# One strided DMA for four in collecting the FFN rows, and the one-hot pieces two and three steps sooner

## The chip, the cores and the metric

The kernel runs on one core of a Trainium2 chip. The metric is the device time of one execution in microseconds, as the median of several runs; the kernel before was run five times. The profile is of one further execution of the same program. Its span runs from the first to the last instruction and is a little shorter than the time of that execution.

The core has five engines with a queue of instructions each, which they work off in order: TensorE (PE in the profile, with its weight loads as PEld), VectorE (DVE), ScalarE (ACT), GpSimd (POOL) and SyncE (SP), which here only issues DMAs. An instruction that needs the result of another engine waits at the head of its queue, and everything behind it on that engine waits too.

## The reference, cut to what matters

`x` is 2048 x 1024 in bfloat16. The output mixes two branches with a gate per row: a linear attention with softmax features over 32 heads of 32 (`a`), and `x` itself with one row changed (`b`). That one row is the row of `x` with the largest routing score `x @ w_r`; a gated feed-forward network (FFN) of width 3584 is applied to it alone.

```python
# attention branch
pq, pk = q @ w_phi, k @ w_phi                                 # per head
phi_q = concat([softmax(pq), softmax(-pq)]); phi_k = concat([softmax(pk), softmax(-pk)])
kv = einsum("bhsf,bhsd->bhfd", phi_k, v); z = phi_k.sum over s
o = einsum("bhqf,bhfd->bhqd", phi_q, kv) / (phi_q . z + 1e-6)
a = o @ wo
# routed branch
r = x @ w_r;  idx = argmax(r)
y = (silu(x[idx] @ w_gate) * (x[idx] @ w_up)) @ w_down * sigmoid(r[idx])
b = x;  b[idx] += y
# mix
g = sigmoid((x * gate_w).sum(-1));  out = g * a + (1 - g) * b
```

## The kernel before, in words

The work goes in three stages.

In the first (to about 70 us) `x` is transposed, `v` is computed (`k_v`, L540), and the per-head matrix `w_phi` is folded into the weights of `q` and `k` (`fold`, L310). `route` finds the row for the FFN.

The second, the k stage (about 70 to 153 us), is a loop written out over `i`, here called steps. Steps 0 to 31 each take one unit `u = i` (128 rows, half of the heads). `k_s0(u)` does eight matmuls `pk` (L582) on PE, two exponentials into a tile `e` on ACT (L585, L586), a sum `ssum` (L590) and reciprocals `rs` (L592) on DVE, a running sum `ksum` on POOL (L594), and the product `phi` (L597), which is on DVE where `u % 4 == 3` and on POOL otherwise. `k_kv(u)` follows five steps later (`LAG`): eight short matmuls `kvps` on PE (L606) that need `phi(u)`. There are four buffers of `e` and six of `phi`. After step 31 the first tiles `pq` of the third stage (L631) take the place of `pk`; they share two PSUM buffers with it. ACT must have read a `pk` or `pq` tile before PE can use its buffer again.

Between these units lie the pieces of the FFN, each at a step given by a number:

- Rounds 0 to 3 of `ffn_gu` (steps 8, 14 and 21, with rounds 2 and 3 both at 21) load gate and up weights through SP (L454) and multiply them with the chosen row: `facc`, L478, leaves four rows of 512 at partitions 0, 32, 64 and 96. ACT copies them to `gs` (L483), and SP sends them to the tile `gT` (L486), in which every row of 512 becomes four rows of 128.
- `ffn_turn(0)` to `(3)` (steps 13, 18, 26 and 27; L439, L442) transpose `gT` by small f32 matmuls into a corner of the PSUM tile `small_ps`. `ffn_mid` (step 27) makes the hidden vector `hh` from it: an exponential on ACT (L446), then L447 to L450 on DVE. `hh32` is its spread copy on ACT (L767, emitted at step 31), which stands on ACT before the exponentials of unit 31.
- `ffn_down` (step 35, L494) multiplies `hh32` with the seven chunks of `w_down`, whose loads (L434) go through SP as soon as buffers are free.
- `one_hot` (step 16: L360 to L367), `one_hot_cols` (step 21: one matmul L372 on PE, then L374 to L385 on DVE) and `one_hot_sums` (step 26: one matmul L390 on PE, then L391 to L397 on DVE) turn the index of the chosen row into a column mask `oh`, the sums `c8` and a clipped index `ixu`, which POOL reads into a register (L831). L372 reads `hlb`, written by L364. L390 reads `csb`, written by L385. L372, L390, L439 and L442 all write parts of the one PSUM tile `small_ps`, and L374 and L391 read it on DVE. The scheduler puts a wait between such an access and the next write of the tile.

The third stage (153 us to the end) computes `pq`, the numerators (`num`, L652), their division on DVE and POOL, the transposes by DMA and the output matmuls (`po`, L709).

The order of the instructions on each engine comes from the Tile scheduler, which interleaves the pieces of neighbouring steps on DVE; the semaphores are set by it too. SP's DMAs take eight completion semaphores in turn, and a DMA whose semaphore is still in use by the DMA eight places before waits for that one to land.

Of the kernel before, what the change touches and what calls it, by code (L numbers as in the profile page):

```python
# [167 lines left out]
def kernel(  # L168
# [4 lines left out]
    nc = tc.nc  # L173
# [54 lines left out]
    gT = const.tile([P, P], F32, name="gT")  # L228
# [85 lines left out]
    def gates():  # L314
        eg = const.tile([P, NT], F32, name="eg")
        nc.scalar.activation(out=eg[:], in_=rg[:, 1, :], func=ACTF.Exp, scale=-1.0)
        nc.vector.tensor_scalar_add(out=eg[:], in0=eg[:], scalar1=1.0)
        nc.vector.reciprocal(out=gate[:], in_=eg[:])
        nc.vector.tensor_scalar(out=omg[:], in0=gate[:], scalar1=-1.0, scalar2=1.0, op0=ALU.mult, op1=ALU.add)
# [117 lines left out]
    def ffn_turn(r):  # L437
        if r < 3:
            nc.tensor.matmul(ffn_ps[:, 16 * r:16 * r + 16], lhsT=gT[:], rhs=identf[:, 0:16], start=True, stop=True)  # L439
        else:  # L440
            for h in range(2):
                nc.tensor.matmul(ffn_ps[:, 48:56], lhsT=gT[:], rhs=identf[:, 16 + 8 * h:24 + 8 * h], start=(h == 0), stop=(h == 1))  # L442
# [9 lines left out]
    def gu_load(r, kp, where):  # L452
        def part(w, a0, src, k0, nk, col, n):
            nc.sync.dma_start(out=w[:, a0:a0 + nk * n * 512].rearrange("p (k f) -> p k f", k=nk) if n == 4 or nk == 4 else  # L454
                              w.rearrange("p (k f) -> p k f", k=2)[:, :, a0:a0 + n * 512],
                              in_=src[:, k0:k0 + nk, col * 512:(col + n) * 512])
        w = wbuf(where)
        gate_load(w[0:1, 0:1])
        k0 = 2 * kp
        if r == 0:  # L460
            part(w, 0, wg_v, k0, 2, 0, 4)
        elif r == 1:
            part(w, 0, wg_v, k0, 2, 4, 3)
            part(w, 1536, wu_v, k0, 2, 0, 1)
        elif r == 2:
            part(w, 0, wu_v, k0, 2, 1, 4)
        else:
            part(w, 0, wu_v, 4 * kp, 4, 5, 2)
        return w

    def ffn_gu(r, bufs):
        ws = [gu_load(r, k, b) for k, b in enumerate(bufs)]
        acc = psB.tile([P, 512], F32, name="facc", tag="pB")
        for k, w in enumerate(ws):
            for q in range(2):
                for g in range(4):
                    kb = 4 * k + 2 * q + g // 2 if r == 3 else 2 * k + q
                    nc.tensor.matmul(acc[32 * g:32 * g + 32, :], lhsT=xs32[:, kb, :],  # L478
                                     rhs=w[:, (q * 4 + g) * 512:(q * 4 + g + 1) * 512], start=(k == 0 and q == 0),
                                     stop=(k == len(ws) - 1 and q == 1),  # L480
                                     tile_position=(0, 32 * g), skip_group_check=True)
        gs = wk.tile([P, 512], F32, name="gs", tag="junk", bufs=2)
        nc.scalar.copy(out=gs[:], in_=acc[:])  # L483
        g0 = 16 if r == 3 else 0
        for g in range(4):
            nc.sync.dma_start(out=gT[g0 + 4 * g:g0 + 4 * g + 4, :], in_=gs[32 * g:32 * g + 1, :])  # L486

    def ffn_down(cs_, pools):
        ws = [wd_load(c, p) for c, p in zip(cs_, pools)]
        for bl in range(4 * len(cs_)):  # L490
            blk = cs_[0] * 4 + bl
            for n in range(2):
                g = (bl % 2) * 2 + n
                nc.tensor.matmul(small_ps[32 * g:32 * g + 32, :], lhsT=hh32[:, blk, :],  # L494
                                 rhs=ws[bl // 4][:, bl % 4, n * 512:(n + 1) * 512], start=(blk < 2),
                                 stop=(blk >= NFB - 2), tile_position=(0, 32 * g), skip_group_check=True)

    def moe_cols():
        ym = ring.tile([P, D * 2], F32, name="ym", tag="wch")
        ys = ym[:, 0:512]  # L500
        y4 = ym[0:KB, 512:768].rearrange("p (s c) -> p s c", s=2)
        yrow = ym[0:1, 768:1280].bitcast(BF)
        ybc = ym[:, 1280:1792].bitcast(BF)
        moe["ybc"] = ybc
        nc.scalar.copy(out=ys, in_=small_ps[:])
        for g in range(4):
            nc.sync.dma_start(out=y4[4 * (g % 2):4 * (g % 2) + 4, g // 2, :], in_=ys[32 * g:32 * g + 1, :])
        moe["y4"] = y4
        moe["yrow"] = yrow
# [67 lines left out]
    def k_s0(u):  # L577
        t, hf = divmod(u, 2)
        pk = psA.tile([P, HH, DH], F32, name="pk", tag="pA")
        pkf = pk[:].rearrange("p h f -> p (h f)")  # L580
        for kb in range(KB):
            nc.tensor.matmul(pkf, lhsT=xT[:, kb, t * P:(t + 1) * P], rhs=wkf[:, kb, hf * 512:(hf + 1) * 512],  # L582
                             start=(kb == 0), stop=(kb == KB - 1))
        e = wk.tile([P, HH, 2, DH], BF, name="e", tag="e", bufs=4)
        nc.scalar.activation(out=e[:, :, 0, :], in_=pk[:], func=ACTF.Exp)  # L585
        nc.scalar.activation(out=e[:, :, 1, :], in_=pk[:], func=ACTF.Exp, scale=-1.0)  # L586
        moe["e"] = e
        e2 = e[:].rearrange("p h s f -> p (h s) f")
        ssum = sm.tile([P, HH * 2], F32, name="ssum", tag="ssum")
        nc.vector.tensor_reduce(out=ssum[:], in_=e2, axis=AX.X, op=ALU.add)  # L590
        rs = sm.tile([P, HH * 2], F32, name="rs", tag="rs")
        nc.vector.reciprocal(out=rs[:], in_=ssum[:])  # L592
        moe["rs"] = rs
        nc.gpsimd.tensor_tensor(out=ksum[:], in0=ksum[:], in1=ssum[:], op=ALU.add)  # L594
        phi = wk.tile([P, HH, 2, DH], BF, name="phi", tag="phi", bufs=6)
        eng = nc.vector if u % 4 == 3 else nc.gpsimd
        eng.tensor_tensor(out=phi[:].rearrange("p h s f -> p (h s) f"), in0=e2,  # L597
                                in1=_bc(rs[:], [P, HH * 2, DH]), op=ALU.mult)
        kst[u] = phi

    def k_kv(u):
        t, hf = divmod(u, 2)
        phi = kst.pop(u)
        for pl in range(NPU):
            pr = hf * NPU + pl
            nc.tensor.matmul(kv_slot(pr),  # L606
                             lhsT=phi[:, 2 * pl:2 * pl + 2, :, :].rearrange("p h s f -> p (h s f)"),
                             rhs=v_all[:, t, hf * HH + 2 * pl:hf * HH + 2 * pl + 2, :].rearrange("p h d -> p (h d)"),
                             start=False, stop=(t == NT - 1), skip_group_check=True)
# [14 lines left out]
    def q_front(sb, j):  # L624
        if j == 0:
            ep = w16 if sb % 2 == 0 else qp["eb"]
            est[sb] = ep.tile([P, KB, 2, SB], BF, name="E", tag="w16" if sb % 2 == 0 else "E")
        E = est[sb]
        pq = psA.tile([P, SB], F32, name="pq", tag="pA")
        for kb in range(KB):  # L630
            nc.tensor.matmul(pq[:], lhsT=wqf[:, kb, j * P:(j + 1) * P], rhs=xT[:, kb, sb * SB:(sb + 1) * SB],  # L631
                             start=(kb == 0), stop=(kb == KB - 1))
        nc.scalar.activation(out=E[:, j, 0, :], in_=pq[:], func=ACTF.Exp)  # L633
        nc.scalar.activation(out=E[:, j, 1, :], in_=pq[:], func=ACTF.Exp, scale=-1.0)
# [124 lines left out]
    for i in range(NU + LAG):  # L759
        if i in GU:  # L760
            r = GU.index(i)
            ffn_gu(r, ("AAAD", "DWVA", "AADD")[r])
            if r == 2:
                ffn_gu(3, "WV")
        if i == NU - 1:
            nc.scalar.copy(out=hh32[0:1, 0, 0:1], in_=moe["e"][0:1, 0, 1, 0:1])
            nc.scalar.copy(out=hh32[:], in_=hh[:].unsqueeze(2).to_broadcast([P, NFB, 32]))  # L767
        if i == DN:
            ffn_down(range(7), "AAADDWV")
            moe_cols()  # L770
        if i >= NU and i - NU < NPRE:
            q_front(0, i - NU)
        if i >= LAG:
            k_kv(i - LAG)
        if i < NU:
            k_s0(i)
        if i == 2:
            gates()
        if i in TU:
            ffn_turn(TU.index(i))  # L780
            if i == TU[3]:
                ffn_mid()
        if i == 6:
            xs_turn()
        if i == 16:
            one_hot()
        if i == 21:
            one_hot_cols()
        if i == 26:
            one_hot_sums()  # L790
    qp["eb"] = None
    kv_finish(range(8), nc.vector.tensor_copy)
# [9 lines left out]
    i = 0  # L802
    while i < n_front + NL + 2 or wq_:
# [3 lines left out]
        if 0 <= n < NU:  # L807
            sb, r = divmod(n, 8)
# [63 lines left out]
```

## Time and profile before

| | |
|---|---|
| median of 5 runs | 278.61 us (278.2 to 279.08) |
| profiled execution | 278.27 us, span 276.6 us, granted TensorE clock 1.000 |
| PE busy | 270.6 us (98% of the span) |
| DVE, POOL, ACT busy | 189.5 us (69%), 141.8 us (51%), 119.2 us (43%) |
| DMA, mean over the span | 173 GB/s, 47.97 MB |

In the profile, "busy" is the time in which an engine has an instruction in execution. A line of a timeline gives the start, the duration, the engine, the line of the kernel, the operation, the written and read tiles and their shapes, how many instructions were merged into it, and in brackets how long the engine had been idle and what ended that. SPq lines are DMA issues on SyncE's queue. Records overlap a little where an instruction starts before the last one has drained, so the distance between starts is often the better measure of what one costs.

### The profile page before, as it was taken

What the parts mean: (1) busy time and instruction counts of PE and PEld (TensorE: products, weight loads), DVE (VectorE), ACT (ScalarE), POOL (GpSimd) and SP (SyncE); (2) the same over time, 40 slices, a digit from 0 to 9 for tenths busy, and PEclk for the clock granted to TensorE, in tenths of its full rate; (3) what the DMA queues carried; (4) which work ended last, traced back from release to release, by engine and by line L of the source; (5) the groups of instructions that cost most, each with busy time, mean ns of one, the idle gap of its engine ahead of it and who ended that gap; (6) DMA issues with size and microseconds to landing.
All of it is one profiled execution on the core that took longest, in us unless ns stands there. A gap on an engine that the chain in (4) does not pass through costs nothing.

```text
span 276.6 us, 5433 instructions
## 1 busy us (share of the span) xinstructions
PE 270.6 (98%) x2023; PEld 149.6 (54%) x2023; DVE 189.5 (69%) x392; ACT 119.2 (43%) x227; POOL 141.8 (51%) x152
## 2 busy tenths in 40 slices
PE   8999999999999999999999999999999999999993
PEld 3666667676544555555454555555455545555442
DVE  3020025556899897999992788888776668899862
ACT  3143332323364646546463647844544554232300
POOL 8000000000097978947953079999756655788310
PEclk9999999999999999999999999999999999999999
DMA  7899999977953797649900528743897255426632
GB/s 257 209 171 191 175 193 293 165 148 217 366 220 107 261 347 280 235 153 339 394 24 4 172 62 298 178 93 13 30 169 214 71 116 118 119 89 140 146 99 63
DMA packets 68767, 47.97 MB, mean 173 GB/s; under 512 B 51376, under 2 KB 56576, under 8 KB 68736
## 3 DMA queue, kind: packets, MB, share of 16 engines
q1 hardware_dynamic: 68240, 47.10, 65.8%
q10 hardware_dynamic: 464, 0.48, 0.5%
q8 instruction: 17, 0.28, 0.4%
q14 instruction: 14, 0.11, 0.1%
q0 software_dynamic: 32, 0.00, 0.0%
HBM read 31.00 MB, written 4.20 MB: 127 GB/s over the span
## 4 chain that ended last, share of the span: by engine, by line
PE 92%; DVE 4%; issue 1%; DMA 1%; ACT 0%; DVEq 0%
PE pq L631 20%; PE po L709 20%; PE pv L540 18%; PE pk L582 16%; PE num L652 6%; PE pW L310 3%; PE kvps L606 3%; PE facc L478 2%; DVE ssum L590 2%; PE pv L562 1%; DMA xs_t<-in_A_x_dram 1%; PE kvps L562 1%; PE small_ps L494 1%; DVE hlc L375 1%; PE pT L291 0%
## 5 line engine op out<-in xcount | busy, mean ns | idle before, releaser
L582 PE MATMUL pk<-wkf,xT 128*128 128x512 bf16 x256 | 60.4, 379 | 0.0
L631 PE MATMUL pq<-xT,wqf 128*128 128x512 bf16 x256 | 60.3, 379 | 0.0
L709 PE MATMUL po<-wo_sb,oT 128*128 128x512 bf16 (+2 forms) x264 | 58.8, 373 | 0.0
L681 POOL TENSOR_TENSOR U<-T 128x512 f32<-128x512 f32 x32 | 41.5, 1297 | 32.1 <-DVE T L666 16.9
L540 PE MATMUL pv<-wv_sb,xT 128*128 128x256 bf16 (+2 forms) x336 | 52.9, 307 | 0.0
L597 POOL TENSOR_TENSOR phi<-e,rs 128x1024 bf16<-128x1024 bf16 x24 | 45.8, 1911 | 2.4 <-DVE rs L592 0.9
L709 PEld LDWEIGHTS <-oT 128*128 128x128 bf16 x264 | 25.4, 98 | 27.8
L590 DVE TENSOR_REDUCE ssum<-e 128x32 f32<-128x1024 bf16 x32 | 38.0, 1191 | 2.8 <-ACT e L586 2.6
L540 PEld LDWEIGHTS <-xT 128*128 128x128 bf16 x336 | 31.5, 97 | 14.6
L666 DVE TENSOR_TENSOR T<-num,rq 128x1024 f32<-128x1024 f32 x32 | 38.8, 1213 | 0.0
L547 ACT CAST v_all<-pv 128x384 bf16<-128x384 f32 (+1 forms) x45 | 20.1, 447 | 41.8 <-PE pv L540 36.0
L631 PEld LDWEIGHTS <-wqf 128*128 128x128 bf16 x256 | 23.8, 98 | 24.1 <-issue 0.6
L712 DVE SCALAR_TENSOR_TENSOR o_out<-po,gate,xg 128x512 bf16<-128x512 f32 (+2 forms) x33 | 23.9, 728 | 17.6 <-PE po L709 16.5
L582 PEld LDWEIGHTS <-xT 128*128 128x128 bf16 x256 | 23.0, 97 | 22.8
L682 POOL TENSOR_TENSOR o_sb<-U,rden 128x512 bf16<-128x512 f32 x32 | 33.5, 1048 | 2.5
L585 ACT ACTIVATE e<-pk 128x512 bf16<-128x512 f32 x32 | 19.1, 597 | 31.0 <-PE pk L582 22.7
L633 ACT ACTIVATE E<-pq 128x512 bf16<-128x512 f32 x32 | 19.0, 595 | 29.2 <-PE pq L631 28.8
L420 POOL COPY wch<-wT 1x1 bf16<-1x1 bf16 x3 | 0.4, 176 | 56.8 <-DMA wT<-in_A_wqkv_dram 56.8
L594 POOL TENSOR_TENSOR ksum<-ksum,ssum 128x32 f32<-128x32 f32 x32 | 14.0, 437 | 22.2 <-DVE ssum L590 17.1
L652 PEld LDWEIGHTS <-E 128*128 128x128 bf16 x256 | 16.4, 98 | 9.3 <-DVE T L666 5.4
L652 PE MATMUL num<-KV,E 128*128 128x136 bf16 x256 | 20.5, 223 | 0.0
L586 ACT ACTIVATE e<-pk 128x512 bf16<-128x512 f32 x32 | 18.9, 591 | 0.0
(137 smaller groups left out, 253.6 us busy)
## 6 DMA issues: line engine op xcount, KB each, us to landing
wch<-in_B_w_down_dram SPq DMA_DIRECT2D x7, 1024.0 KB
wch<-in_B_w_up_dram SPq DMA_DIRECT2D x6, 1024.0 KB
wch<-in_B_w_gate_dram SPq DMA_DIRECT2D x4, 1024.0 KB
xin<-in_A_x_dram SPq DMA_DIRECT2D x16, 256.0 KB
out_dram<-o_out SPq DMA_DIRECT2D x30, 128.0 KB
wch<-in_B_w_gate_dram SPq DMA_DIRECT2D x4, 768.0 KB
wv_sb<-in_A_wqkv_dram SPq DMA_DIRECT2D x8, 256.0 KB
wo_sb<-in_A_wo_dram SPq DMA_DIRECT2D x1, 2048.0 KB
```

The costliest lines, as they stand in the source:

```text
L540: nc.tensor.matmul(pv[:, 0:hi - lo], lhsT=xT[:, kb, t * P:(t + 1) * P], rhs=wv_sb[:, kb, lo:hi], start=(kb == 0), stop=(kb == KB - 1))
L547: nc.scalar.copy(out=v_all[:, t, h0:h1, 0:DH], in_=pv[:, 0:(h1 - h0) * DH].rearrange("p (h d) -> p h d", d=DH))
L582: nc.tensor.matmul(pkf, lhsT=xT[:, kb, t * P:(t + 1) * P], rhs=wkf[:, kb, hf * 512:(hf + 1) * 512], start=(kb == 0), stop=(kb == KB - 1))
L590: nc.vector.tensor_reduce(out=ssum[:], in_=e2, axis=AX.X, op=ALU.add)
L597: eng.tensor_tensor(out=phi[:].rearrange("p h s f -> p (h s) f"), in0=e2, in1=_bc(rs[:], [P, HH * 2, DH]), op=ALU.mult)
L631: nc.tensor.matmul(pq[:], lhsT=wqf[:, kb, j * P:(j + 1) * P], rhs=xT[:, kb, sb * SB:(sb + 1) * SB], start=(kb == 0), stop=(kb == KB - 1))
L652: nc.tensor.matmul(num[:, b * NSTR:b * NSTR + KVW], lhsT=E[:, j, sg, tl * P:(tl + 1) * P], rhs=KV[hf][:, sg, jl, :], start=True, stop=True)
L666: nc.vector.tensor_tensor(out=T[:].rearrange("p s (j h) d -> p (s j) h d", h=4), in0=nv[:, :, :, 0:DH], in1=rS.unsqueeze(3).to_broadcast([ ...
L681: nc.gpsimd.tensor_tensor(out=U[:], in0=T[:, 0], in1=T[:, 1], op=ALU.add)
L682: nc.gpsimd.tensor_tensor(out=st["o"][:, hf * HH:(hf + 1) * HH, :], in0=U[:], in1=_bc(rden[:], [P, HH, DH]), op=ALU.mult)
L709: nc.tensor.matmul(po[:, 0:w], lhsT=st["oT"][:, kb, :], rhs=moe["wo"][:, kb, sl], start=(kb == 0), stop=(kb == KB - 1))
L712: nc.vector.scalar_tensor_tensor(out=o_out[:, 0:w], in0=po[:, 0:w], scalar=gate[:, t:t + 1], in1=st["xg"][:, sl], op0=ALU.mult, op1=ALU.add)
```

## The change

Two things are edited. In `ffn_gu`, rounds 1 to 3 send their four rows to `gT` by one DMA whose source steps over partitions 0, 32, 64 and 96; round 0 keeps four DMAs of one row each. `one_hot_cols` moves from step 21 to step 19, and `one_hot_sums` from step 26 to step 23. The number of matmuls and of instructions on DVE, ACT and POOL stays the same; SP issues nine DMAs fewer. From L486 on, every line number in the changed file is one higher.

```diff
@@ -482,8 +482,9 @@
         gs = wk.tile([P, 512], F32, name="gs", tag="junk", bufs=2)
         nc.scalar.copy(out=gs[:], in_=acc[:])
         g0 = 16 if r == 3 else 0
-        for g in range(4):
-            nc.sync.dma_start(out=gT[g0 + 4 * g:g0 + 4 * g + 4, :], in_=gs[32 * g:32 * g + 1, :])
+        step = 4 if r >= 1 else 1
+        for g in range(0, 4, step):
+            nc.sync.dma_start(out=gT[g0 + 4 * g:g0 + 4 * (g + step), :], in_=gs[32 * g:32 * (g + step):32, :])
 
     def ffn_down(cs_, pools):
         ws = [wd_load(c, p) for c, p in zip(cs_, pools)]
@@ -784,9 +785,9 @@
             xs_turn()
         if i == 16:
             one_hot()
-        if i == 21:
+        if i == 19:
             one_hot_cols()
-        if i == 26:
+        if i == 23:
             one_hot_sums()
     qp["eb"] = None
     kv_finish(range(8), nc.vector.tensor_copy)
```

## The prediction

> **What bounds the kernel now.** I read the page's busy row first, then the chain of waits, then the timeline of each engine through the k stage.
>
> ```profile
> PE 270.6 (98%) x2023; PEld 149.6 (54%) x2023; DVE 189.5 (69%) x392; ACT 119.2 (43%) x227; POOL 141.8 (51%) x152
> ```
>
> PE is busy for 98% of the span at full clock. Only a PE idle stretch that goes, or a new one, can move the end. The chain of waits runs along PE everywhere after the start except from 120.5 to 132.9 us, where it follows DVE from L374 to L391 and comes back to PE at L442. PE's timeline shows the one hole there:
>
> ```profile
> 111.37 0.29 PE L439 MATMUL small_ps<-identf,gT 128*128 128x16 f32 x2
> 111.51 0.41 PE L606 MATMUL kvps<-v_all,phi 128*128 128x66 bf16 x8
> ...
> 130.19 0.29 PE L439 MATMUL small_ps<-identf,gT 128*128 128x16 f32 x2
> 130.33 0.16 PE L390 MATMUL small_ps<-csb,const-bfloat16-1.0 128*128 128x2 bf16 x1
> 130.36 0.41 PE L606 MATMUL kvps<-v_all,phi 128*128 128x66 bf16 x8
> 130.61 1.89 PE L582 MATMUL pk<-wkf,xT 128*128 128x512 bf16 x8
> 132.94 0.61 PE L442 MATMUL small_ps<-identf,gT 128*128 128x8 f32 x4 [0.44 <-DVE c L391]
> 133.41 0.41 PE L606 MATMUL kvps<-v_all,phi 128*128 128x66 bf16 x8
> ```
>
> L442 (step 27) writes `small_ps`, which L391 (step 26) has to read first. L391 stands on DVE behind two sums; L390, whose result it copies, starts at 130.33, so DVE is 2.4 us behind PE here. DVE's lines, then POOL's:
>
> ```profile
> 112.97 0.51 DVE L364 CAST hlb<-hl 1x2 bf16<-1x2 uint32 x1
> ...
> 116.95 1.76 DVE L597 TENSOR_TENSOR phi<-e,rs 128x1024 bf16<-128x1024 bf16 x1
> ...
> 120.69 1.71 DVE L375 TENSOR_TENSOR hlc<-hlc,iot 128x1 f32<-128x1 f32 x1
> ...
> 131.68 1.16 DVE L590 TENSOR_REDUCE ssum<-e 128x32 f32<-128x1024 bf16 x1
> 132.75 0.13 DVE L391 COPY c<-small_ps 8x2 f32<-8x2 f32 x1
> 132.94 0.35 DVE L592 RECIPROCAL rs<-ssum 128x32 f32<-128x32 f32 x1
> ```
>
> ```profile
> 111.55 1.91 POOL L597 TENSOR_TENSOR phi<-e,rs 128x1024 bf16<-128x1024 bf16 x1 [0.23 <-PE pk L582]
> ...
> 113.64 1.91 POOL L597 TENSOR_TENSOR phi<-e,rs 128x1024 bf16<-128x1024 bf16 x1
> ...
> 115.72 1.91 POOL L597 TENSOR_TENSOR phi<-e,rs 128x1024 bf16<-128x1024 bf16 x1
> ...
> 120.47 1.91 POOL L597 TENSOR_TENSOR phi<-e,rs 128x1024 bf16<-128x1024 bf16 x1 [0.23 <-PE small_ps L372]
> ```
>
> L375 handles one element per partition and takes 1.71 us: it ends at 122.40, when POOL's `phi` ends (120.47 + 1.91 = 122.38). L364 ends at 113.48, with the `phi` that ends at 113.46. DVE's `phi` at 116.95 ends 1.08 after POOL's (115.72 + 1.91 = 117.63), though the same form needs only 1.15 where POOL is idle (138.40). So some DVE forms wait for the end of a POOL operation, and get in before the next one.
>
> **Part one, the DMAs.**
>
> ```profile
> 102.18 2.48 SPq L486 DMA_DIRECT2D gT<-gs  x4
> ...
> 118.14 5.00 SPq L486 DMA_DIRECT2D gT<-gs  x8
> 123.23 4.80 SPq L434 DMA_DIRECT2D wch<-in_B_w_down_dram  x5
> ```
>
> One issue takes 0.57 to 0.73 us. Round 1 frees SP 2.48 - 0.6 = 1.9 us sooner. For rounds 2 and 3 SP sends one at 118.14, waits for the second `gs` (118.39 + 0.59 = 118.98) and sends the other, so the five `w_down` loads start at about 119.7, 3.5 us sooner. Nobody waits for any of it. `gT` of round 1 is read at 111.37, 7 us after the last issue; rounds 2 and 3 at 130.19, 7 us after. L494 uses `w_down` at 147.36, while DMA is at 0.72 of its time in 134 to 141 us (5 us of it, so loads end near 139) and at 0.01 in 141 to 153: 8 us of cover. A strided DMA of 16 rows isn't in the trace. Between the 0.57 of one row and the 1.24 of a transposing issue I take 0.6; in either case the cover holds, and the price is 0. Nor do its new waits cost: round 1's DMA now waits for round 0's landings, which write the same rows (issued 88.2 to 90.8, over 11 us earlier), round 2's for round 1's (15 us earlier). With nine DMAs fewer, later ones wait for other predecessors on their semaphore (two `w_down` loads for round 3's weights, which `facc` has read by then; the fifth for the load issued at 105.8). Price 0; bounds 0 and, if one load waited for such a neighbour, still 0 by the 8 us.
>
> **Part two, the pieces moved.** The built order of the changed kernel tells where each lands.
>
> *The hole at L442 goes.* L390 and L391 now stand at step 23, and L391 is done near 125, so L442 no longer waits for it. Without a wait L442 starts 1.73 after its `pk` (as 109.64 to 111.37): 130.61 + 1.73 = 132.34. Its four records take 0.28, as two take 111.51 - 111.37 = 0.14, so `kvps` starts at 132.62 in place of 133.41: **-0.79**. The chain's own step (132.94 - 132.34 = 0.60) is the lower bound.
>
> *L372 two steps sooner.* It now follows the `pk` of step 19, so it could start at 113.49, where `kvps` starts now, but needs `hlb`, which L364 ends at 113.48. DVE to PE takes 0.06 (L391 ends 132.88, L442 at 132.94): 113.54. Behind it PE has weight loads of `kvps` that it could not start ahead; eight take 0.32 after the unhindered L372 and 0.50 otherwise. Bounds 0.03 and 0.3; I take **+0.1**, near the first, since the wait itself is 0.05. L390 at step 23 needs `csb` (near 121) at 124.3: 0.
>
> *DVE around step 19.* L374 to L385 came at 120.5 to 125.0, while `facc` of rounds 2 and 3 (2.7 us of PE, no DVE) had let DVE catch up. Now they come at 114.9. L375 waits for POOL's `phi` to end at 115.55, not 1.7 us but 0.2. L376 follows (0.3), then L378, also a product of two SBUF tiles, meets the next `phi` (115.72 to 117.63): 1.7 us lost there. The sum of unit 19 is behind it, at 117.7 in place of 115.30. Then POOL has nothing to do, since its next `phi` needs the sum of unit 20, so L379 goes free and DVE's `phi` takes 1.15, not 1.76. Unit 20's `rs` comes at 122.0 (before 119.94), unit 21's at 123.5 (before 124.58), because the one-hot work is behind DVE by then. POOL's `phi` of unit 20 ends near 124.4, 1.6 before its `kvps` loads (126.0); units 21 and 22 near 126.5 and 128.6, 1.5 before theirs. No wait on PE: 0. If all three products each lost a `phi`, 1.0 to 1.4 us of lag would go on to `kvps` of unit 24 and cost up to 0.5; that is my upper bound.
>
> The Trainium skill (SBUF — State Buffer, section on the two separate sides) calls the port pair of VectorE and GpSimd an exclusive lock, held for a whole instruction, with the loser blocked. It speaks against this move: taken alone, each of L375, L378, L379 put beside a busy POOL costs up to the 1.91 of a `phi`, 5.7 us of DVE, against 1.9 by the rows above, since POOL itself runs dry behind the blocked DVE.
>
> *L395 and POOL's L831* (reads `ixu` from L397). L395 now stands right after unit 24's `rs`, and POOL's `phi` needs 0.17 after that `rs`, so L395 gets in: 0.15. L397 ends near 133, L831 comes after `phi` of unit 25, near 136: 0.
>
> *After the hole.* PE runs 0.7 sooner into POOL's products. `phi` of units 24 to 26 end 1.5 before their `kvps` now; with DVE and POOL 0.4 sooner themselves and PE 0.7, 1.2 is left. What is late next is ACT:
>
> ```profile
> 140.94 0.94 ACT L767 COPY hh<-hh 128x896 bf16<-128x896 bf16 x1
> ...
> 142.28 0.59 ACT L586 ACTIVATE e<-pk 128x512 bf16<-128x512 f32 x1
> ```
>
> `pq` at 143.31 needs the buffer that this L586 frees at 142.87. At 143.31 - 0.7 = 142.61 it would wait 0.3, unless L767, which waits for L447 to L450 on DVE, comes sooner too. DVE is 0.4 ahead, and free of L395's 0.71, so I expect 0, bound 0.3. Then PE sets the pace to the end.
>
> **Sum** against the profiled execution: -0.79 + 0.1 = -0.7, 278.27 to 277.6 (span 275.9). The median of the runs is 0.34 above the profiled one, so the median goes from 278.61 to **277.9**.
>
> **Rivals.**
>
> *Thinner covers take half.* The blocked products hold DVE for longer, or L447 misses its gap between two POOL operations, and PE waits 0.3 at `pq` or up to 0.5 at `kvps` of unit 24 to 26. For it: POOL's cycle of four steps (three `phi` at 2.08, and a fourth turn lost to DVE's) is as long as PE's four steps (4 x 1.98), so lag isn't made up. Against: the margins of 1.2. Time: 278.61 - 0.7 + 0.35 = 278.3.
>
> *Nothing changes.* L442 finds another late predecessor, and the chain goes back to DVE: 278.6. Against: in the built order L442 has no wait on DVE left, and the next matmul's is for `phi` of unit 23, done near 130.
>
> *Slower: L372 waits a whole `phi`.* If POOL's next `phi` (113.64) gets in ahead of L364, `hlb` comes at 113.64 + 1.91 = 115.55, and PE idles 2.1 us at step 19: 278.61 - 0.8 + 2.1 = 279.9. It decides if L364 comes to DVE 0.2 us later. For it: L364 had 6.8 us of cover at step 21 and has none now. Against: nothing in front of L364 is changed, and in this trace it got in. A milder form is L395 losing to the `phi` of unit 24 (2 us of DVE lag, some 1.3 on PE): 279.2.
>
> **How the numbers follow.** About 0.2% (0.56 us) can be told from no change. Full gain 0.55, half 0.22, nothing 0.10, slower 0.13. The full gain of 0.7, within 0.6 to 0.8, passes 0.56 in some three of four runs of the comparison, so faster 0.45; the rest of it, half and nothing make same 0.42; slower 0.13. The range starts at 277.5 (0.79, and the runs' own scatter) and goes to 279.0, over the half and nothing cases and the scatter; 279.2 and beyond is left out. The likeliest case's own range is 277.5 to 278.2.
>
> **What would show it.** Right: L442 starts 1.73 after its `pk` with no idle; L375 short and L378 some 1.9 long near 115.7; three single L486 issues, `w_down` issued from about 119.7, and L494 not moved by it; all of PE after step 27 sooner by 0.7. Wrong: a PE idle before L372 or behind it near 113.5 of over 0.3, before `kvps` of units 20 to 26, or before the second `pq`; or L442 idle again.

## The result and the profile after

The changed kernel takes 277.58 us in the median of 31 runs (276.93 to 278.97), beside 278.57 us for the kernel before in 53 runs (278.04 to 279.56). The ratio is 0.997 with a 95% interval of 0.9962 to 0.9978: 0.84 us faster, between 0.6 and 1.06. The profiled execution took 277.36 us with a span of 275.7 us, against 278.27 and 276.6 before. From L486 on, line numbers are one higher than before wherever the DMA loop has its added line.

The busy row and the chain of waits of the changed kernel, from its page:

```profile
PE 270.6 (98%) x2023; PEld 149.9 (54%) x2023; DVE 189.7 (69%) x392; ACT 119.3 (43%) x227; POOL 140.8 (51%) x152
...
PE 97%; DMA 1%; ACT 0%; DVE 0%; issue 0%
```

PE is busy for the same 270.6 us. In the chain PE had 92% before and DVE 4%; now DVE has 0%. The timeline of PE shows why (start, duration, engine, line):

```profile
111.46 0.29 PE L439 MATMUL small_ps<-identf,gT 128*128 128x16 f32 x2
111.60 0.41 PE L607 MATMUL kvps<-v_all,phi 128*128 128x66 bf16 x8
111.85 1.89 PE L583 MATMUL pk<-wkf,xT 128*128 128x512 bf16 x8
113.63 0.16 PE L372 MATMUL small_ps<-hlb,const-bfloat16-1.0 128*128 128x2 bf16 x1
113.66 0.41 PE L607 MATMUL kvps<-v_all,phi 128*128 128x66 bf16 x8
...
130.75 1.89 PE L583 MATMUL pk<-wkf,xT 128*128 128x512 bf16 x8
132.48 0.51 PE L442 MATMUL small_ps<-identf,gT 128*128 128x8 f32 x4
132.84 0.41 PE L607 MATMUL kvps<-v_all,phi 128*128 128x66 bf16 x8
...
142.75 1.89 PE L632 MATMUL pq<-xT,wqf 128*128 128x512 bf16 x8
```

L442 starts 132.48 - 130.75 = 1.73 after its `pk`, with no idle in front of it; before it was 2.33. From that `pk` to `kvps` PE takes 2.09 in place of 2.80: -0.71. With L372 in front of it `kvps` starts 113.66 - 111.85 = 1.81 after its `pk`; the same pair was 1.73 apart before (111.76 and 113.49): +0.08. From L439 at step 18 to the second `pq` it is 142.75 - 111.46 = 31.29 against 143.31 - 111.37 = 31.94 before: **-0.65**. All of that stands at the end: the last additions into `o_out` start 271.15 - 111.46 = 159.69 after L439, against 160.36 before. This stretch will serve as the measure of PE below, since it is free of what an execution adds at its start and end. With nothing in it edited it came out at 31.95 in the first experiment (31.94 before); but the changed kernel, run again without an edit, gave 31.38, so differences under 0.1 us say little.

What is left of the 0.9 between the two spans lies behind the last additions: from their start to the end of the span it took 276.6 - 271.73 = 4.87 before and takes 275.7 - 271.15 = 4.55 now. The last three experiments ask what that is.

DVE of the changed kernel around step 19, then POOL beside it:

```profile
113.07 0.51 DVE L364 CAST hlb<-hl 1x2 bf16<-1x2 uint32 x1
...
115.39 0.26 DVE L375 TENSOR_TENSOR hlc<-hlc,iot 128x1 f32<-128x1 f32 x1
115.69 2.06 DVE L376 TENSOR_SCALAR oh<-iot,hlc 128x16 f32<-128x16 f32 x1
117.78 0.18 DVE L378 TENSOR_TENSOR oh<-oh,er 128x16 f32<-128x16 f32 x1
...
119.00 0.17 DVE L379 TENSOR_TENSOR oh<-oh,omg 128x16 f32<-128x16 f32 x1
...
124.99 0.14 DVE L391 COPY c<-small_ps 8x2 f32<-8x2 f32 x1
...
131.27 0.08 DVE L395 TENSOR_TENSOR ixm<-ixm,ixf 1x1 f32<-1x1 f32 x1
...
135.69 1.93 DVE L447 TENSOR_SCALAR sg<-sg 128x28 f32<-128x28 f32 x1
```

```profile
113.73 1.91 POOL L598 TENSOR_TENSOR phi<-e,rs 128x1024 bf16<-128x1024 bf16 x1
...
115.81 1.91 POOL L598 TENSOR_TENSOR phi<-e,rs 128x1024 bf16<-128x1024 bf16 x1
...
122.56 1.91 POOL L598 TENSOR_TENSOR phi<-e,rs 128x1024 bf16<-128x1024 bf16 x1 [0.23 <-DVE rs L593]
```

One of the small one-hot instructions loses a whole POOL product: L376 takes 2.06 us, until 117.75, where the product that began at 115.81 ends at 117.72. L391 is done at 125.13, more than 5 us before the next write of `small_ps` on PE.

SP's queue with the strided DMAs:

```profile
118.30 1.40 SPq L487 DMA_DIRECT2D gT<-gs  x2
119.79 4.85 SPq L434 DMA_DIRECT2D wch<-in_B_w_down_dram  x5
```

### The profile page after: what moved, and what is told of

It is laid out like the page before. It is cut to its first block, busy times and chain, and to the rows that moved or that the text cites. A ratio compares the mean times of both kernels' runs of the same rounds, so it can differ in the third digit from the quotient of the medians.

```text
span 275.7 us, 5413 instructions
## 1 busy us (share of the span) xinstructions
PE 270.6 (98%) x2023; PEld 149.9 (54%) x2023; DVE 189.7 (69%) x392; ACT 119.3 (43%) x227; POOL 140.8 (51%) x152
## 4 chain that ended last, share of the span: by engine, by line
PE 97%; DMA 1%; ACT 0%; DVE 0%; issue 0%
PE pq L632 20%; PE po L710 20%; PE pk L583 20%; PE pv L541 18%; PE num L653 6%; PE kvps L607 3%; PE pW L310 3%; PE facc L478 2%; PE pv L563 1%; PE kvps L563 1%; DMA xs_t<-in_A_x_dram 1%; PE small_ps L495 1%; PE pT L291 1%; ACT xT L292 0%; DVE o_out L713 0%; PE small_ps L439 0%
## 5 line engine op out<-in xcount | busy, mean ns | idle before, releaser
L595 POOL TENSOR_TENSOR ksum<-ksum,ssum 128x32 f32<-128x32 f32 x32 | 13.0, 408 | 22.8 <-DVE ssum L591 17.2
```

## The experiments

The measure of time is the median beside that of the kernel before in the same rounds; PE's stretch is L439 (step 18) to the second `pq` in one profiled execution. "End" runs from SP's last store issue to the last of the eight waits in which SP collects the landings. The ratio is not that of the two medians (those of `e12` give 0.9964, the ratio is 0.9975); where the two disagree, the text goes by the ratio and its interval.

| kernel | columns, sums at | gT DMAs | us (before) | ratio, 95% | PE's stretch | end |
|---|---|---|---|---|---|---|
| before | 21, 26 | 16 | 278.57 | | 31.94 | 2.3 |
| changed | 19, 23 | 7 | 277.58 (278.57) | 0.997, 0.9962 to 0.9978 | 31.29 | 1.9 |
| e1_dma_only | 21, 26 | 7 | 278.32 (278.69) | 0.9995, 0.9978 to 1.0012 | 31.95 | 2.0 |
| e2_moves_only | 19, 23 | 16 | 277.93 (278.69) | 0.997, 0.9957 to 0.9983 | 31.29 | 3.0 |
| e3_sums25 | 21, 25 | 16 | 279.68 (278.69) | 1.0032, 1.0016 to 1.0048 | 32.54 | 3.2 |
| e4_cols18 | 18, 23 | 7 | 278.74 (278.69) | 1.0008, 0.9992 to 1.0024 | 32.37 | 2.0 |
| e7_sums24 | 21, 24 | 16 | 278.28 (278.63) | 0.9983, 0.9969 to 0.9997 | 31.62 | 3.3 |
| e5_sums33 | 21, 33 | 16 | 281.88 (278.63) | 1.0081, 1.0048 to 1.0114 | 31.21 | 2.6 |
| e6_cols19_only | 19, 26 | 16 | 277.99 (278.63) | 0.9965, 0.9948 to 0.9982 | 31.39 | 3.3 |
| e9_psum | 21, 26 | 16 | 278.69 (278.63) | 1.0, 0.998 to 1.0019 | 31.64 | 2.9 |
| e8_cols20_sums23 | 20, 23 | 7 | 277.47 (278.44) | 0.9962, 0.9949 to 0.9975 | 31.21 | 2.0 |
| e10_after_again | 19, 23 | 7 | 277.62 (278.44) | 0.9963, 0.9947 to 0.9979 | 31.38 | 2.0 |
| e11_eight_fewer | 19, 23 | 8 | 278.05 (278.49) | 0.9989, 0.9972 to 1.0006 | 31.29 | 3.2 |
| e12_one_fewer | 19, 23 | 15 | 277.50 (278.49) | 0.9975, 0.9954 to 0.9996 | 31.30 | 2.0 |

### The two parts alone

`e1_dma_only` has the strided DMAs and leaves the one-hot pieces at 21 and 26; `e2_moves_only` has the moves and the sixteen single DMAs.

```diff
e1:
-        if i == 19:
+        if i == 21:
             one_hot_cols()
-        if i == 23:
+        if i == 26:
             one_hot_sums()
```

> The change's DMA part alone: rounds 1 to 3 by one strided DMA, the one-hot pieces back at steps 21 and 26. Theory (the hole at L442 is the whole gain): the time is that of before, 278.6 within 0.2; L442 still starts some 0.6 us after its pk could let it, waiting for L391; the w_down loads are issued near 119.8 and L494 is not moved. Rival (the DMAs give part of the gain, for instance the 0.3 us by which the changed kernel's span shrank behind its last DVE operation): 278.3, that is 0.2 to 0.35 less, with L442 still waiting.

> The other part alone: one_hot_cols at step 19 and one_hot_sums at step 23, sixteen DMAs as before. Theory: the time of the changed kernel, 277.7 within 0.2; L442 without a wait, L372 some 0.1 us late. Rival (DMAs give part): 278.0 to 278.1.

PE's stretch is 31.95 with the DMAs alone and 31.29 with the moves alone. So all of the 0.65 on PE comes from the moves. In time `e1` cannot be told from before by its ratio, though its median lies where the rival had it, at 278.3. `e2` has the same stretch as the changed kernel and the same ratio of 0.997, yet its median is 0.35 longer than the changed kernel's. The runs on the end take that up.

### Moving the sums alone: step 25, 24 and 33

```diff
-        if i == 26:
+        if i == 25:     # e3; 24 in e7, 33 in e5
             one_hot_sums()
```

> Before, with one_hot_sums one step sooner (25 in place of 26) and nothing else. Theory (it is only that L391 is read in time before L442; moving one_hot_cols is not needed): L390 near 128.2, L391 near 131.3, L442 without a wait at 1.73 us after its pk; without the cost at L372, 277.7 to 277.8, as fast as the change or 0.1 faster. Rival (DVE must be relieved by the earlier one_hot_cols, or the hole turns up elsewhere): L391 again after 132.3 or a new PE idle, 278.4 to 278.8.

> The kernel before with the sums (L390 to L397) at step 24 in place of 26, the columns left at 21, the sixteen single DMAs kept. My theory: what costs before's hole is only that L391 comes after the next write of small_ps on PE, and moving the sums pays when L391 gets in front of DVE's own product phi (128.10 in the trace of before) and of PE's turn at 130.19. csb is ready at 124.96 and PE passes step 24 near 126.3, so L390 waits for nothing, L391 is done near 127.9, neither L439 nor L442 waits, and L372 keeps its old place: -0.7 to -0.8, about 277.9, ratio 0.997, as fast as the whole change or 0.1 faster. Rival (the columns must be moved too, since at step 21 they still hold DVE back, as with the sums at 25): L391 again ends after 130.2, a wait of 1 at L439, 279.3 to 279.7.

> The kernel before with the sums at step 33, behind all the turns, in place of 26; all else as before. My theory: no write of small_ps on PE stands behind L391 any more, so L442 and L439 wait for nothing and the hole goes from the other side: PE L442 1.73 behind its pk, -0.7 to -0.8, about 277.9, ratio 0.997. Rival: L390 now waits for the reads of small_ps by L447 to L450 (140.4 in the trace of before) or L494 for c8, and PE loses 0.2 to 1 there: 278.1 to 278.9.

At 25 the kernel became slower. PE in the profile of `e3_sums25`:

```profile
128.41 0.17 PE L390 MATMUL small_ps<-csb,const-bfloat16-1.0 128*128 128x2 bf16 x1
...
131.62 0.40 PE L439 MATMUL small_ps<-identf,gT 128*128 128x16 f32 x2 [1.03 <-DVE c L391]
```

DVE in the same profile:

```profile
128.30 2.07 DVE L597 TENSOR_TENSOR phi<-e,rs 128x1024 bf16<-128x1024 bf16 x1
130.29 1.21 DVE L590 TENSOR_REDUCE ssum<-e 128x32 f32<-128x1024 bf16 x1
131.42 0.14 DVE L391 COPY c<-small_ps 8x2 f32<-8x2 f32 x1
```

L390 is two microseconds sooner on PE, but L391 runs at 131.42, since on DVE it still stands behind the product `phi` of unit 23 and the sum after it. The matmul that waits is now L439 of step 26, one turn earlier, and PE loses 1.03 in place of 0.44. My expectation had looked at L442 alone.

At 24 L391 gets in front of that product, and the hole goes. PE in the profile of `e7_sums24`:

```profile
126.30 0.17 PE L390 MATMUL small_ps<-csb,const-bfloat16-1.0 128*128 128x2 bf16 x1
...
130.29 0.29 PE L439 MATMUL small_ps<-identf,gT 128*128 128x16 f32 x2
...
132.41 0.51 PE L442 MATMUL small_ps<-identf,gT 128*128 128x8 f32 x4
...
143.06 1.89 PE L631 MATMUL pq<-xT,wqf 128*128 128x512 bf16 x8 [0.23 <-ACT e L586]
```

Yet only 0.32 of PE's 0.65 arrives: the second `pq` waits for ACT to empty its buffer. It starts 2.37 behind the first where 1.98 is the rule. With the columns left at 21, DVE isn't ahead: `hh` (L450) starts 129.39 us after the L439 of step 18, where the changed kernel has 128.89. So the spread copy of `hh` on ACT and the exponential behind it come too late.

At 33 the stretch to the second `pq` is the shortest, 31.21, but the bill comes behind it. PE in the profile of `e5_sums33`, with the first 20 of the 56 matmuls of L494:

```profile
149.50 1.85 PE L494 MATMUL small_ps<-wch,hh 128*32 128x512 bf16 x20 [2.37 <-DVE c L391]
```

L494 writes the same tile, and L391 stands on DVE behind a minimum (L678) that waits 1.95 for POOL and a `phi` after it, so that it starts at 149.30:

```profile
147.65 0.19 DVE L678 TENSOR_REDUCE rmn<-ksum 128x1 f32<-128x32 f32 x1 [1.95 <-POOL ksum L594]
...
149.30 0.14 DVE L391 COPY c<-small_ps 8x2 f32<-8x2 f32 x1
```

PE idles for 2.37 us there. More is lost right behind it. From about 150.0 to 153.4 us the profile's granted TensorE clock is 0.50 (1.00 before and after), and the 56 matmuls of L494 take 4.82 us to the start of the next `pq`, where they took 3.14 in the kernel before. After the shorter idles of 0.44, 0.97 and 1.03 us (before, `e4`, `e3`) the clock stayed at 1.00. That the long idle brought the lower clock is the likely reading, but it is one profile. By the last additions `e5` is 3.44 us behind the kernel before. My rival named the waiting L494 as one of its two places, and had the price at 0.2 to 1.

### Moving the columns: 19 alone, 18, 20

```diff
-        if i == 21:
+        if i == 19:     # e6, sums left at 26; e4 and e8: 18 and 20, with sums at 23
             one_hot_cols()
```

> The kernel before with the columns (L372 to L385) at step 19 in place of 21, the sums left at 26, sixteen DMAs kept. My theory: L391 still stands between the sums on DVE right in front of L442, so the hole stays, smaller only by what DVE is ahead: in the trace of the changed kernel DVE's sum of the unit is 0.2 sooner (131.49 against 131.68), with less in front of it 0.4 to 0.6; so L442 still waits 0 to 0.4 and L372 costs 0.1: -0.1 to -0.5, 278.1 to 278.5, ratio 0.998 to 1.0. Rival (DVE's one-hot work of steps 21 to 25 is the cause, not the place of L391): the whole gain, 277.9.

> The change, with one_hot_cols at step 18 in place of 19. Theory (L372 at step 19 stands just behind the moment when hlb is ready, so one step more makes PE wait): L372 could start near 111.6, L364 ends near 113.5, so PE idles 1.9 to 2.0 us at step 18 and the time is the change's plus that, 279.4 to 279.7. Rival (the scheduler brings L364 forward or PE makes the wait good later): within 0.5 us of the change, 277.6 to 278.1.

> The changed kernel with the columns at step 20 in place of 19 (sums at 23, strided DMAs). L372 then has 2 us of cover for hlb and its weights. My theory: from the turn at step 18 (L439 near 111.4) to the second pq of the next stage, the trace of before shows 31.94, of the changed kernel 31.29; without any wait or added record it is about 31.2. So the 0.08 that L372 costs at step 19 goes, 31.2, in time 0.1 below the changed kernel, which the times cannot tell. Rival: the columns at 20 leave DVE less ahead, as the columns at 21 did (with the sums at 24 the second pq waited 0.23 for ACT and the stretch was 31.62): 31.4 to 31.6, 0.1 to 0.3 above the changed kernel.

My theory missed on `e6`: the columns alone give nearly all of it, 0.55 of PE's 0.65. PE in its profile, then DVE:

```profile
131.29 1.89 PE L582 MATMUL pk<-wkf,xT 128*128 128x512 bf16 x7
133.01 0.60 PE L442 MATMUL small_ps<-identf,gT 128*128 128x8 f32 x4
133.47 0.41 PE L606 MATMUL kvps<-v_all,phi 128*128 128x66 bf16 x8
```

```profile
131.74 1.16 DVE L590 TENSOR_REDUCE ssum<-e 128x32 f32<-128x1024 bf16 x1
132.82 0.13 DVE L391 COPY c<-small_ps 8x2 f32<-8x2 f32 x1
```

L391 still stands behind the sum of unit 25 and still releases L442, but that sum now starts 0.45 behind PE's `pk` (131.74 - 131.29), where before it was 1.07 (131.68 - 130.61). DVE is 0.6 us further ahead of PE, and L442 starts 1.72 behind its `pk`, just in time. So the hole was not only a matter of where L391 stands; it was as much DVE's lag, and the one-hot work at steps 21 to 25 made part of that lag. At step 19 this work lies in the stretch where PE spends 2.7 us on `facc`, which asks nothing of DVE. Either move can take the hole away (the sums do it at 24, not at 25); the columns also keep the second `pq` from waiting.

At 18, L372 comes to PE before `hlb` is there. PE in the profile of `e4_cols18`:

```profile
113.86 0.16 PE L372 MATMUL small_ps<-hlb,const-bfloat16-1.0 128*128 128x2 bf16 x1 [0.97 <-DVE hlb L364]
```

The stretch is 1.08 longer than the changed kernel's, and the time takes back the gain (ratio 1.0008 where the changed kernel has 0.997). I had expected 1.9 to 2.0. The schedule had put L372 between the third and the fourth matmul of the next `pk`, so part of the wait lay beside work.

At 20, L372 costs nothing. The stretch is 31.21, as expected, and it is the shortest of all kernels that pay nothing later (last additions 159.64 after L439), though by no more than the changed kernel's own two executions differ. That L372 is free here shows directly: the next matmuls start 1.82 behind their `pk`, as in the kernel before. Its median of 277.47 is the lowest, but it cannot be told from the changed kernel's 277.62 in the same rounds.

### Which forms wait for POOL

```diff
-        nc.vector.tensor_tensor(out=hlc[:, 1:2], in0=hlc[:, 1:2], in1=iot[:, NT:NT + 1], op=ALU.is_equal)
+        nc.vector.tensor_tensor(out=hlc[:, 1:2], in0=cb_ps[:, 1:2], in1=iot[:, NT:NT + 1], op=ALU.is_equal)
```

> The kernel before with L375 reading its first operand from PSUM (cb_ps) in place of SBUF; the result is the same. It asks which forms wait for POOL's phi. In the trace of before L375 (two SBUF operands, 1 element) takes 1.71, beside POOL's phi of 120.47 to 122.38. My theory: two SBUF operands, or an SBUF operand and two scalars from SBUF in float32, take the port and wait; with one operand in PSUM L375 takes about 0.16, and L376 behind it waits in its place, 1.4 to 1.6. Time the same, within 0.2 of before. Rival: any form waits, whatever its operands: L375 stays at 1.7 and L376 at 0.29. Second rival: only forms with two SBUF tensors wait, and L376 takes 0.2 to 0.3, L378 the 1.3.

DVE in the profile of `e9_psum`, beside a `phi` on POOL from 120.89 to 122.80:

```profile
121.11 0.16 DVE L375 TENSOR_TENSOR hlc<-small_ps,iot 128x1 f32<-128x1 f32 x1
121.31 1.53 DVE L376 TENSOR_SCALAR oh<-iot,hlc 128x16 f32<-128x16 f32 x1
122.87 0.18 DVE L378 TENSOR_TENSOR oh<-oh,er 128x16 f32<-128x16 f32 x1
```

With one operand in PSUM L375 takes 0.16 where it took 1.71, and L376, which reads one tile and two scalars from SBUF, waits in its place. So the wait is a matter of the operands, not of the size: L376 handles 16 elements. Nor does it need scalars in SBUF, as my theory had it. L447, which reads one SBUF tile and a constant, took 1.93 in the changed kernel, until POOL's `phi` of 135.68 was done. The cast L385, with one SBUF tile, took 1.56 in `e8_cols20_sums23`, from 121.23 until the `phi` that ended at 122.76; it took 0.11 in the kernel before. Since L375 no longer has its turn behind the wait, L378 starts 0.3 sooner against POOL, and PE's stretch shrank by 0.30 with it; the time doesn't show that.

### The end of the kernel

`e10_after_again` is the changed kernel without an edit. `e11` and `e12` are the changed kernel but for how many DMAs bring the rows to `gT`:

```diff
-        step = 4 if r >= 1 else 1
+        step = (1, 4, 4, 2)[r]                                    # e11: 8 DMAs
-        for g in range(0, 4, step):
+        for g, step in ((0, 2), (2, 1), (3, 1)) if r == 3 else ((0, 1), (1, 1), (2, 1), (3, 1)):    # e12: 15 DMAs
```

> The changed kernel again, without an edit, beside the kernel before and the run with the columns at 20. My theory: what the change gives is the 0.65 of PE's stretch from L439 to the second pq, and what the first comparison showed beyond it (0.84 in the medians, 0.9 in the profiled spans) is the scatter of the landing of the last store and of the start: the stretch again 31.29, the time 0.6 to 0.9 below before. Rival: the strided DMAs give another 0.2 in time at the start or the end of the kernel, which shows again as a span of 275.7 or less at full clock while the stretch stays at 31.29.

> The changed kernel (columns at 19, sums at 23) with rounds 1 and 2 sent by one strided DMA and round 3 by two of two rows each: 8 DMAs in place of 16, where the changed kernel has 7. It asks for the end of the kernel. In the five profiles with 7 DMAs, from SP's last store issue to the last of its eight waits for landings takes 1.9 to 2.0 us; in the seven profiles with 16 it takes 2.3 to 3.3. PE's stretch from L439 to the second pq as in the changed kernel, 31.3 to 31.4. Theory A (fewer DMAs as such): 8 is as good as 7, the end takes 2.0, time 277.5 to 277.7. Theory B (SP waits for its landings at eight places in turn; nine DMAs fewer put the last stores one place further, eight fewer leave them where they were): the end takes 2.3 to 3.3 as with 16, time 277.9 to 278.1. Theory C (scatter): somewhere between, with no relation.

> The changed kernel (columns at 19, sums at 23) with single DMAs in all rounds but for two rows of round 3 that leave together: 15 DMAs, one fewer than 16. PE's stretch from L439 to the second pq 31.3 to 31.4. Theory A (the number of DMAs): 15 is as bad as 16, the end from SP's last store issue to its last wait takes 2.3 to 3.3, time 277.9 to 278.1. Theory B (the place of the last stores among eight): one fewer is as good as nine fewer, the end takes 2.0, time 277.5 to 277.7. Theory C (scatter): no relation.

SP's waits behind the last store and their starts in the profile of `e11_eight_fewer` (in the first line: us in total, times, longest; in the second, after the count and the length in ns, the starts of the first and the last), then the packets of ACT's queue q10 in the stretches 273 to 274, 274.3 to 274.7 and 274.7 to 275.1 us:

```profile
SPq L840 <- SPq L840: 2.3, 3, 1.3
...
L840 SPq EVENT_SEMAPHORE  x8: 17/17/17, 274.0 to 275.5; - x8
```

```profile
q10 hardware_dynamic: 141, 0.08, 27.8%
...
q10 hardware_dynamic: 6, 0.00, 5.5%
...
q10 hardware_dynamic: 3, 0.00, 3.4%
```

The same in the profile of `e12_one_fewer`; its q10 has 150 packets in 273 to 274 us and none after:

```profile
SPq L839 <- SPq L839: 1.2, 3, 0.5
...
L839 SPq EVENT_SEMAPHORE  x8: 17/17/17, 273.3 to 274.4; - x8
```

```profile
q10 hardware_dynamic: 150, 0.09, 29.9%
```

With 8 DMAs the last wait comes 3.2 behind SP's last store issue (272.3 to 275.5), with 15 it is 2.0 (272.4 to 274.4). Fewer DMAs are no help as such. With 7 and 15 the end takes 1.9 to 2.0 in all six profiles, with 8 and 16 it takes 2.3 to 3.3 in all eight. From the last additions to the end of the span it is 4.55 to 4.65 us in the six and 4.87 to 5.89 in the eight. Theory B foretold this from the place of the last stores among SP's eight semaphores. But only numbers one below a multiple of eight and multiples of eight were run, so odd against even would fit as well, and that the place is the cause isn't shown.

The medians go the same way. The four sets with columns at 19 or 20, sums at 23 and 7 or 15 DMAs have 277.47 to 277.62; the three that have columns at 19 and 8 or 16 DMAs have 277.93 to 278.05. The ratios don't separate the two groups: they are 0.9962 to 0.9975 and 0.9965 to 0.9989. So a step of 0.3 to 0.5 us in time rests on seven medians from different rounds, and only the step in the profiled ends is clear.

In `e11`, nine of the 144 packets of ACT's last store come up to 1 us after the others, and SP's last wait is behind them. (The last two stores on q10 have 288 packets between them; six of the 150 in 273 to 274 us belong to the store before.) The profile of before, with an end of 2.3, has no such latecomers in its last store, and in `e12` the store before the last has nine, from 272.5 to 273.4 us, and its end is short all the same. What makes packets late isn't shown. So the 0.32 by which the end of the profiled execution shrank is not mere scatter, as I had held until then: it goes with the DMA part of the change.

`e10` itself bore out neither of its expectations in full. The stretch was 31.38 and not 31.29, since `kvps` behind L372 came 0.16 late and not 0.08, and the span was 276.0, above the rival's 275.7. The gain came again: the medians are 0.82 apart.

The Trainium skill (DMA: Bandwidth & Descriptors, section on queues, rings and completion order) says that one copy is split over up to 16 DMA engines and that a completion increment lands only behind the earlier writes of its engine, so the slowest engine sets the landing. The nine late packets of the 144 in `e11` agree with that; that the number of copies before it matters, the page doesn't say.

## Why the prediction was right, and where it was not

*The size and sign.* It said 277.9, a gain of 0.7. The medians give 277.58, and the ratio a gain of 0.84. By the trace the sum is -0.65 on PE, where the prediction had -0.7, and -0.32 at the end, where it had 0. That the median lies 0.32 below the 277.9 is of the size of that end.

*The hole at L442: right, with half of the reason.* L442 started 1.73 behind its `pk`, as said. The term was -0.79 and measured -0.71, because the four f32 records take 132.84 - 132.48 = 0.36, not 0.28: twice what two take did not hold. By the profile the weight loads set the pace: they take 0.63 for four and 0.41 for two, and in both cases the next `kvps` starts 0.05 before their end. The step gave the whole gain to the new place of L391 and none to DVE's lag. The runs show that columns at 19 with L391 left in its old place give 0.55 of the 0.65, and sums at 24 with the columns left give 0.32, because the hole goes there too but the second `pq` then waits.

*L372 at step 19: right.* +0.1 was taken and +0.08 measured; a second execution had 1.89 between `pk` and `kvps`, +0.16. Both lie between the bounds of 0.03 and 0.3. L364 ended with POOL's `phi` each time.

*DVE around step 19: the amount right, the instruction wrong.* L375 was short (0.26), and one `phi` was lost. But L376 lost it, not L378: the prediction had taken only products of two SBUF tiles for forms that wait. The trace of before couldn't show otherwise: there L376 met no running `phi`. The times came out all the same: `rs` of unit 20 at 122.03 (said 122.0), of unit 21 at 123.57 (123.5), and POOL's `phi` of unit 20 ended at 122.56 + 1.91 = 124.47 (124.4). The estimate that the prediction drew from the skill's rule, 5.7 us of DVE against its own 1.9, was too high for this place. One of the four instructions lost a whole product, some 1.8 us over the 0.29 that L376 took before.

*L395, L397 and the end of the stage: right, by a margin.* L395 took 0.08. L447 missed its gap between two products on POOL and took 1.93, which the prediction had as a rival's mishap; it cost nothing, since `pq` at 142.75 starts 1.99 behind the one before it. That cover is thin, though: with the columns at 21 the second `pq` does wait (`e7`), so the "thinner covers" rival describes a neighbour of this change and not the change itself.

*The DMA part: wrong by its reason.* Its steps on SP hold: two issues in 1.40 us, `w_down` from 119.79 (said 119.7), and PE's stretch doesn't move. "Price 0; bounds 0" failed at a place that the prediction never looked at, the landings of the last stores, and so did its opening sentence that only an idle stretch of PE can move the end. There the profiled execution gained 0.32, and all fourteen profiles part by the number of DMAs; by the medians it is 0.3 to 0.5 us, which the ratios don't confirm. The prediction had noticed that later DMAs get other neighbours on their semaphore, and priced only the `w_down` loads.

*The slower rival* was real one step away: with the columns at 18 PE waits 0.97 for `hlb`, and the gain is gone. The nearest slower kernel was another, though, sums at 25, where the wait passes to the matmul before.

## What to carry to other kernels

When an instruction is moved off a wait, look for the next writer of the same tile on each side of its new place; what counts is where its reader stands in its own engine's order, not where its producer does. Work of a lagging engine goes best into a stretch where the bounding engine does something that asks nothing of it. A change in the number of DMAs should be looked for at the end of the kernel as well, in the landings of the last stores. Behind a long idle of the bounding engine look at the granted clock too, as in `e5`.

## What the runs showed of the hardware that was not expected

- A DVE instruction with one SBUF tile can wait for a running POOL product as one with two does: L376 (16 elements) took 2.06 and 1.53 us against 0.19 to 0.29, L447 (28 elements) 1.93, the cast L385 1.56 against 0.11. L375 with an operand in PSUM doesn't (0.16 against 1.71). The Trainium skill (SBUF — State Buffer, section on who interferes with whom) names two SBUF inputs, and casts and `tensor_scalar` where their operands fit a two-port mode; both agree with these rows.
- Four f32 matmuls of 128 x 8 behind one another take 0.36, and their weight loads 0.63 in the profile, so a pair's 0.14 can't be doubled.
- After PE had been idle for 2.37 us in `e5`, its granted clock was 0.50 for some 3.4 us of work, and 56 matmuls took 4.82 us in place of 3.14. After idles of up to 1.03 us it stayed at 1.00.
- The end of the kernel goes with the number of small DMAs issued over 150 us before it: 3.2 us with 8 and 2.0 with 15, in two kernels that differ only in how the rows reach `gT`. Why isn't shown.
